# Fewer TensorE transposes of x, halved and paced loads, and tail groups that keep their own PSUM tile, in a fused attention and channel-mix kernel

## The chip, the cores and the metric

The kernel runs on one core of a Trainium2 chip. The metric is the time of one execution on the device in microseconds (us); lower is better. Executions of one kernel vary by about one per cent, so each comparison below uses several runs, with the kernel before run on the same chip in the same rounds. A run is called slow when it lies more than 1.5% above the fastest of the same kernel; ratios use the other ("fast") runs.

Engine names as the profile has them: PE is TensorE (matmul), PEld its weight loads, DVE is VectorE, ACT is ScalarE, POOL is GpSimd, SP is SyncE. A "q" behind an engine's name (SPq, POOLq) means its sequencer, which also issues DMAs.

## The reference, cut to what matters

```python
# q, k, v: (8, 8, 576, 64); features 128; d_model 512; d_ff 1024
def phi(x):
    proj = x @ w_phi
    proj = proj - max(abs(proj), axis=-1)
    return concat([exp(proj), exp(-proj)])
q_p, k_p = phi(q), phi(k)
x = (q_p @ (k_p^T v)) / (q_p @ sum(k_p) + 1e-6)      # heads side by side: (8, 576, 512)

x_prev = x shifted by one position
xk = mu_k * x + (1 - mu_k) * x_prev
xr = mu_r * x + (1 - mu_r) * x_prev
k = relu(xk @ w_k); v = (k * k) @ w_v; r = sigmoid(xr @ w_r)
out = r * v                                           # (8, 576, 512)
```

## The kernel before: the parts that matter here

The work is cut into 32 pairs of heads (four for each of eight batches), one tail group for each batch (three for the first; the ninth of the nine slices of 64 positions, for all heads together), and the channel mix of each batch. Each small operation has a name, and one long list of words says in which order they are emitted. Every engine and every DMA queue does its share in exactly this order. `kp20` is the projection of k of pair 20, `mh20` the copies of its maxima, `xz20` the DMA transposition of its x, `xu20` the copy behind it, `lk6.0` a load of k of batch 6. A suffix picks the engine (`/DVE`) or a PSUM tile (`:1`).

```python
ORDER = """
...
h2.1:1 rk15 kc14/ACT h2.2:0 nd13:2 rd13 xz13 xz13.d:0 lk6.0 rl2.1/ACT sq2.1/POOL mh15 rl2.2/ACT
sq2.2/POOL r2.0:1 th2.0 tr18 h2.3:0 so1.3.d:0 mt15:1 tr17 qp16:2 qp17:1 mc15/DVE rl2.3/ACT lq6.0
lv6.0 ka15 ea15 eb15 h2.4:0 h2.5:1 rq16 rq17 sq2.3/POOL rl2.4/ACT xu12/POOL df12/POOL qt15:2 qa15
...
"""
```

PSUM holds three tiles of two banks ("P", for projections, kv, nd) and two of one bank ("M", for h, r, v and small transposes). A tail group projects k and q into a P tile, has the maxima reduced on VectorE, copied on GpSimd (`mhe`), transposed by TensorE (`mte`), and then corrected by a matmul (`kae`) in the first bank. Its q part lies in an M tile:

```python
def mte():
    s["pm"] = pm = motile(("mo", "m" + tag), "ps_me")          # an M tile
    nc.tensor.transpose(pm[:, 0:64].bitcast(BF), mh, ident)
def kae():                                                      # the correction, bank 0 of the P tile
    nc.tensor.matmul(s["ps"][:, 0, 0:n * 128], lhsT=s["mT"][0:64, :],
                     rhs=sel[0:64, 0:n, :].rearrange("p a f -> p (a f)"),
                     start=False, stop=True, skip_group_check=True)
def qte():
    s["pq"] = ps = motile(("mo", "q" + tag), "ps_qe")           # another M tile
    ...
def eqe():                                                      # two exponentials from it (ACT)
    ...
    nc.scalar.activation(t[:, a0:a1, 64:192], s["pq"][:, 0:n * 128]..., AF.Exp, scale=...)
```

The output x of a pair reaches the channel mix transposed. Pairs 0 to 7 are transposed by TensorE, later ones by a DMA, behind which a 63-column copy shifts the edge:

```python
XPE = 8
def xz():
    nc.sync.dma_start_transpose(out=xs[:, a, :]..., in_=s["x"]...)
def xu(eng):
    copy(eng, xs[:, a, 1:64], xs[:, a, 576:639])
def mix(i):                                                     # always VectorE
    nc.vector.scalar_tensor_tensor(out=t[:, a, ...], in0=s["d"], scalar=mu[:, a:a + 1],
                                   in1=xs[:, a, 0:S], op0=ALU.mult, op1=ALU.add)
```

GpSimd issues all loads (q, k and v of a batch whole, 576 KB each, from batch 2 on), copies the maxima (`mhx`), and shares diffs and squares with VectorE and ScalarE.

## Time and profile before

| | before |
|---|---|
| time, median of 3 | 305.64 us (304.15 to 306.35) |
| profiled execution | span 304.2 us, mean granted clock 0.986 |
| TensorE / VectorE / ScalarE / GpSimd busy | 278.4 / 240.3 / 223.3 / 127.4 us |
| first h matmul starts | 51.9 us |

TensorE bounds the kernel, so the question in every stretch is what TensorE waits for. The prediction below shows the lines and how to read them. One more view: what TensorE's idle times ended with (line waited for, then us in total, times, longest). The kernel before has two of over 1.5 us in all:

```profile
PE ps_me L476 <- POOL mhlt L471: 3.5, 3, 2.4
PE ps_m L589 <- DVE ob L818: 1.6, 1, 1.6
```

What stands in no such line is the half rate after a gap and the crumbs too short to be listed.

### The profile page before, as it was taken

How to read it: one execution, taken by the hardware profiler on the slowest of the kernel's cores; microseconds unless marked ns; L12 is line 12 of the kernel's file. 1: busy time of each engine (PE TensorE's matmuls, PEld its weight loads, DVE VectorE, ACT ScalarE, POOL GpSimd, SP SyncE). 2: the span in 40 equal slices, each digit the busy share in tenths (PEclk: the TensorE clock that was granted, in tenths of full speed). 3: DMA queues.
4: the chain of work that ended last, by engine and by line, in shares of the span. 5: the costliest groups of instructions: out<-in, count | busy, mean ns of one | idle time of the engine just before them, and what ended most of it. 6: DMA issues, size and time to landing. Idle time of an engine off the chain costs nothing.

```text
span 304.2 us, 9054 instructions
## 1 busy us (share of the span) xinstructions
PE 278.4 (92%) x3765; PEld 158.4 (52%) x3813; DVE 240.3 (79%) x369; ACT 223.3 (73%) x408; POOL 127.4 (42%) x261
## 2 busy tenths in 40 slices
PE   6688798999899999969999997999999999999993
PEld 2456465565456655534555654454556655554541
DVE  5776789979978999667978988799869888777331
ACT  3397899998689897855888884898797878923410
POOL 7763533696047346653443714353034403400400
PEclk9999989999999999998999999999999999999999
DMA  8999957399989957996957898913924364233125
GB/s 152 204 209 207 169 83 105 59 194 206 194 174 128 148 124 131 197 200 113 177 110 107 145 125 157 162 47 61 187 60 69 11 93 94 58 74 71 39 58 116
DMA packets 66137, 38.18 MB, mean 126 GB/s; under 512 B 47024, under 2 KB 60720, under 8 KB 66096
## 3 DMA queue, kind: packets, MB, share of 16 engines
q1 hardware_dynamic: 51280, 20.82, 39.4%
q0 software_dynamic: 14672, 16.48, 35.1%
q8 instruction: 30, 0.49, 0.7%
q10 hardware_dynamic: 144, 0.29, 0.3%
q14 instruction: 11, 0.09, 0.1%
HBM read 33.62 MB, written 9.44 MB: 142 GB/s over the span
## 4 chain that ended last, share of the span: by engine, by line
PE 61%; DVE 18%; DMA 7%; ACT 6%; issue 3%; POOL 2%; SPq 1%; DVEq 0%; POOLq 0%
PE ps_v L812 14%; PE ps_h L779 13%; PE ps_r L798 7%; PE ps_nd L656 5%; DMA xs<-x_sc 4%; PE ps_kv L635 4%; DVE nm L565 4%; DVE nm L560 3%; DVE xk L706 2%; PE ps_ve L896 2%; ACT q L620 2%; PE ps_he L866 2%; DVE xr L706 2%; PE ps_q L548 2%; PE ps_k L598 2%
## 5 line engine op out<-in xcount | busy, mean ns | idle before, releaser
L620 ACT ACTIVATE q<-ps_qT 128x512 bf16<-128x512 f32 x128 | 67.1, 622 | 3.0 <-PE ps_qT L612 2.8
L575 ACT ACTIVATE k<-ps_k 128x1024 bf16<-128x1024 f32 x64 | 62.9, 1038 | 5.6 <-PE ps_k L598 4.3
L779 PE MATMUL ps_h<-xk,wk_bf 128*128 128x512 bf16 x237 | 60.8, 379 | 1.3 <-issue 0.3
L812 PE MATMUL ps_v<-wv_bf,kk 128*128 128x512 bf16 x243 | 58.2, 379 | 1.0 <-issue 0.3
L565 DVE TENSOR_REDUCE nm<-ps_q 128x8 f32<-128x1024 f32 x32 | 38.7, 1218 | 4.3 <-PE ps_q L548 4.1
L560 DVE TENSOR_REDUCE nm<-ps_k 128x8 f32<-128x1024 f32 x32 | 38.8, 1217 | 3.8 <-PE ps_k L548 3.8
L812 PEld LDWEIGHTS <-kk 128*128 128x128 bf16 x256 | 23.9, 98 | 28.8 <-issue 1.9
L211 POOL TENSOR_TENSOR kk<-krelu 128x512 bf16<-128x512 bf16 x23 | 23.9, 1047 | 35.4 <-DVE krelu L205 21.7
L779 PEld LDWEIGHTS <-wk_bf 128*128 128x128 bf16 x256 | 22.5, 97 | 25.2 <-issue 2.3
L584 POOL CAST mhl<-nm 128x16 bf16<-128x16 f32 x32 | 8.0, 250 | 64.1 <-DVE nm L560 64.0
L798 PE MATMUL ps_r<-wr_bf,xr 128*128 128x512 bf16 x118 | 32.9, 394 | 1.2 <-issue 0.5
L804 ACT ACTIVATE rt<-ps_r 128x512 bf16<-128x512 f32 x32 | 19.5, 609 | 18.0 <-PE ps_r L798 15.7
L700 POOL TENSOR_TENSOR diff<-xs 128x576 bf16<-128x576 bf16 x21 | 28.0, 1336 | 7.6 <-DVE xs L682 2.8
L203 ACT ACTIVATE krelu<-ps_h 128x512 bf16<-128x512 f32 x39 | 23.2, 611 | 10.1 <-PE ps_h L779 8.3
L706 DVE SCALAR_TENSOR_TENSOR xk<-diff,mu_k_t,xs 128x576 bf16<-128x576 bf16 x32 | 28.5, 892 | 1.3 <-POOL diff L700 1.0
L818 DVE SCALAR_TENSOR_TENSOR ob<-rt,ps_v 128x512 f32<-128x512 bf16 x32 | 21.8, 682 | 8.7 <-PE ps_v L812 4.2
L666 DVE TENSOR_TENSOR x_sc<-ps_nd,rden 128x640 bf16<-128x640 f32 x32 | 26.4, 825 | 1.1
L706 DVE SCALAR_TENSOR_TENSOR xr<-diff,mu_r_t,xs 128x576 bf16<-128x576 bf16 x32 | 26.9, 840 | 0.0
L548 PEld LDWEIGHTS <-qkT 64*128 64x128 bf16 x512 | 17.6, 94 | 12.0 <-issue 9.7
L635 PE MATMUL ps_kv<-v,k 64*128 64x65 bf16 x1024 | 22.8, 192 | 0.6 <-ACT q L620 0.4
L635 PEld LDWEIGHTS <-k 64*128 64x128 bf16 x1024 | 19.9, 95 | 5.1 <-issue 3.8
L205 DVE TENSOR_SCALAR krelu<-ps_h 128x512 bf16<-128x512 f32 x25 | 17.1, 688 | 6.6 <-PE ps_h L779 6.0
(99 smaller groups left out, 467.5 us busy)
## 6 DMA issues: line engine op xcount, KB each, us to landing
out_dram<-ob SPq DMA_DIRECT2D x72, 128.0 KB, 2.4
nat<-in_k_dram POOLq DMA_DIRECT2D x6, 576.0 KB, 8.6
nat<-in_q_dram POOLq DMA_DIRECT2D x6, 576.0 KB, 8.9
vt<-in_v_dram POOLq DMA_DIRECT2D x6, 576.0 KB, 9.6
wk_bf<-in_moe_w_k_dram POOLq DMA_DIRECT2D x2, 512.0 KB, 10.8
wv_bf<-in_moe_w_v_dram POOLq DMA_DIRECT2D x2, 512.0 KB, 12.3
nat<-in_k_dram POOLq DMA_DIRECT2D x3, 288.0 KB, 7.4
nat<-in_q_dram POOLq DMA_DIRECT2D x3, 288.0 KB, 7.3
```

Source lines behind the costliest of these rows:

```text
L211: (nc.vector if eng == "DVE" else nc.gpsimd).tensor_tensor(out_, in_, in_, op=ALU.mult)
L560: nc.vector.tensor_reduce(s["nm"][:, 0, :], s["k"].rearrange("p a (g f) -> p (a g) f", f=128), axis=AX.X, op=ALU.max, apply_absolute_value ...
L565: nc.vector.tensor_reduce(s["nm"][:, 1, :], s["q"].rearrange("p a (g f) -> p (a g) f", f=128), axis=AX.X, op=ALU.max, apply_absolute_value ...
L575: nc.scalar.activation(s[f"k{pn}"], s["k"].rearrange("p a (g f) -> p (a g) f", f=128), AF.Exp, scale=(1.0 if pn == 0 else -1.0))
L620: nc.scalar.activation(t[:, h, :].rearrange("f (g a p) -> f g a p", g=4, a=2), s["qT"].rearrange("f a (g h p) -> f h g a p", g=4, h=2)[:, ...
L635: nc.tensor.matmul(ps[:, hh, pn * 65:(pn + 1) * 65], lhsT=s[f"k{pn}"][r, c, :], rhs=vb[r, a, 2 * g + par, :], start=(pn == 0 and c == 0), ...
L666: nc.vector.tensor_tensor(s["x"].rearrange("p (b s) d -> p b s d", b=2), ndv[:, :, :, 0:64], s["rd"].to_broadcast([128, 2, 5, 64]), op=ALU ...
L700: (nc.vector if eng == "DVE" else nc.gpsimd).tensor_tensor(s["d"], xs[:, a, 64:64 + S], xs[:, a, 0:S], op=ALU.subtract)
L706: nc.vector.scalar_tensor_tensor(out=t[:, a, (b % 2) * S:(b % 2 + 1) * S], in0=s["d"], scalar=mu[:, a:a + 1], in1=xs[:, a, 0:S], op0=ALU.m ...
L779: nc.tensor.matmul(ps, lhsT=wk_bf[:, c, fc * 128:(fc + 1) * 128], rhs=xkt[bp][:, c, m0:m0 + 512], start=(c == 0), stop=(c == NDC - 1))
L798: nc.tensor.matmul(ps, lhsT=xrt[bp][:, c, m0 + ci * 128:m0 + (ci + 1) * 128], rhs=wr_bf[:, c, :], start=(c == 0), stop=(c == NDC - 1))
L812: nc.tensor.matmul(ps, lhsT=s["kk"][:, fc, ci * 128:(ci + 1) * 128], rhs=wv_bf[:, fc, :], start=(fc == 0), stop=(fc == NFC - 1))
```

## The change

The intent: less work on TensorE and ScalarE, more free PSUM tiles, loads that do not crowd the DMA transposes of x, and engines dealt out anew. The whole order was rewritten with it. Its core:

```diff
+    def pick(eng):
+        return nc.vector if eng == "DVE" else nc.gpsimd
...
-            "kpn": 2, "qpn": 2, "tl": 2, "xk": 2, "kk": 2, "krelu": 3, "rt": 3, "ob": 4,
+            "kpn": 3, "qpn": 3, "tl": 2, "xk": 2, "kk": 2, "krelu": 4, "rt": 4, "ob": 4,
...
+        pace = lambda i: [f"xu{4 * (b - 3) + i + (a0 > 0) * (1 if i > 3 else 2)}"] if b > 3 else []
...
-    lparts = {b: [(0, NP)] for b in range(B)}
+    lparts = {b: [(0, 2), (2, 4)] for b in range(B)}
...
         def mte():
-            s["pm"] = pm = motile(("mo", "m" + tag), "ps_me")
-            nc.tensor.transpose(pm[:, 0:64].bitcast(BF), mh, ident)
+            nc.tensor.transpose(s["ps"][:, 1, 0:64].bitcast(BF), mh, ident)
...
         def qte():
-            s["pq"] = ps = motile(("mo", "q" + tag), "ps_qe")
+            s["pq"] = ps = s["ps"][:, 1, :]
...
-    XPE = 8
+    XPE = 4
...
-                for h in range(2):
-                    nc.scalar.activation(
-                        t[:, h, :].rearrange("f (g a p) -> f g a p", g=4, a=2),
-                        s["qT"].rearrange("f a (g h p) -> f h g a p", g=4, h=2)[:, h],
-                        AF.Exp, scale=(1.0 if pn == 0 else -1.0))
+                nc.scalar.activation(t.rearrange("f j (a p) -> f j a p", a=2),
+                                     s["qT"].rearrange("f a (j p) -> f j a p", p=64),
+                                     AF.Exp, scale=(1.0 if pn == 0 else -1.0))
...
+                if eng == "POOL":
+                    md = small.tile([128, S], FP, name="md", bufs=1)
+                    nc.gpsimd.tensor_scalar(md, s["d"], mu[:, a:a + 1], None, op0=ALU.mult)
+                    nc.gpsimd.tensor_tensor(t[:, a, ...], md, xs[:, a, 0:S], op=ALU.add)
+                    return
...
+        cols = [(0, DM)] if bp < B // 2 - 1 else [(0, DM // 2), (DM // 2, DM)]   # last edge in halves
...
 ORDER: rewritten; for example, a tail group
- mce4.0/ACT ... kae4.0 ... ekt4.0 ... qte4.0:1 ... eqe4.0
+ mce4.0/DVE ... qte4.0 ... eqe4.0 ... kae4.0 ... ekt4.0
```

## The prediction

> **What bounds the kernel now.** I read the busy shares first, then the slices of the span, then the table of windows, then the chain that ended last, and then the order of time where the windows showed a hole. The page:
>
> ```profile
> PE 278.4 (92%) x3765; PEld 158.4 (52%) x3813; DVE 240.3 (79%) x369; ACT 223.3 (73%) x408; POOL 127.4 (42%) x261
> PE   6688798999899999969999997999999999999993
> PEclk9999989999999999998999999999999999999999
> ```
>
> TensorE is the bound: 92% busy, and from slice 7 on nearly always at nine tenths; no other engine passes 79%. But busy is not full speed, so I counted what TensorE had to do. In the chain eight 512-column matmuls take 1.73 us, 216 ns each; a pair's kv takes about 0.6 us, its nd 0.67, eight projections 0.23, one transpose of 128 columns 0.056. Counts times these spacings give 245 us of real work in 304. By windows of 8 us it is 25 us in the first 56 us (so 31 us are lost there), then 7.1 to 7.9 of 8 nearly everywhere, and only 4.9 and 5.9 in the two windows from 128 to 144. From 56 us to the end of the last matmul at 299.3 some 23 us are lost: some 4 us of it in those two windows alone (10.8 us of work where neighbours have 14.7), and the rest in crumbs of half a microsecond per window, with about 1 us extra each at 72, 168, 184 and 200. The table of windows there (columns: TensorE, its weight loads, VectorE, ScalarE, GpSimd, clock, DMA share, GB/s):
>
> ```profile
> 120.00:128.00 8.00, 7.89 (x116) 4.57 (x117) 5.45 (x9) 6.63 (x12) 4.21 (x7) 1.00 1.15 192
> 128.00:136.00 8.00, 5.51 (x103) 3.37 (x103) 5.66 (x8) 4.95 (x11) 4.96 (x10) 0.97 1.24 199
> 136.00:144.00 8.00, 7.51 (x46) 3.18 (x45) 5.88 (x10) 4.81 (x8) 3.08 (x11) 0.82 0.71 117
> ```
>
> And why, from the chain that ended last, and then from the order of time:
>
> ```profile
> 125.10 13.39 DMA xs<-x_sc
> ```
>
> ```profile
> 125.10 18.90 SPq L677 DMA_TRANSPOSE xs<-x_sc  x3
> 131.54 0.23 POOL L199 COPY xs<-xs 128x63 bf16<-128x63 bf16 x1 [2.80 <-DMA xs<-x_sc]
> 134.53 0.23 PE L476 MATMUL ps_me<-ident,mhlt 128*128 128x128 bf16 x1 [2.44 <-POOL mhlt L471]
> 137.98 1.06 PE L798 MATMUL ps_r<-wr_bf,xr 128*128 128x512 bf16 x2 [0.22 <-issue]
> ```
>
> GpSimd issued five whole loads of 576 KB between 117.5 and 127.7 us. In this stretch a transposing DMA of x needed 10.5 us in the median, against 3.5 us over the whole run. GpSimd stood in order behind it, the tail's small copies (mhlt) stood behind GpSimd, and TensorE stood behind those for 2.44 us. Then the clock was halved: the r matmuls that follow are 427 ns apart, for one stretch of 3.4 us.
>
> **What the Trainium skill says.** "DMA: Bandwidth & Descriptors", section "Issuing engines are not separate DMA queues": all DMAs end on the same 16 engines and interleave. The trace agrees: 10.5 against 3.5 us. "TensorE: Matmul & The Clock Gate", Part 1: an idle window of about 3.4 us brings half rate. The trace agrees on the half rate and its 3.4 us, though the visible gap was only 2.44 us. "ScalarE: Activation LUTs", section "What ACT_TABLE_LOAD costs": 186 ns + 0.833 ns per element, with 93 ns overlapped back to back: 612 ns for 512, 1039 for 1024. The trace has 622 and 1038. "GPSIMD Engine Reference", 4.1: operations with two inputs are about twice as slow on GpSimd as on VectorE. Here it is worse: the diff takes 1336 ns against 495.
>
> **The change, part by part.**
>
> (1) x of pairs 4 to 7 goes by DMA. Removed: 20 TensorE transposes, 20 x 0.056 = 1.1 us of work; four evictions, about 0.65 + 0.2 us each on ScalarE or VectorE, 3.4 us. Added: four DMA transposes of 3.5 us, with slack, since batch 1 is mixed only later. On the path: -1.1 us.
>
> (2) Loads of batches 2 to 7 are halved, and those of 4 to 7 stand in GpSimd's order behind the small copies that wait for x transposes landed before. Added: 18 more issues of 0.75 us on GpSimd, 13.5 us, off the path. The queue in front of a transpose becomes half as deep, so the hole at 128 to 144 should close. On the path: -4 us.
>
> (3) The tail groups put their small transpose and their q projection into the second bank of their own tile. This frees the two single banks twice for each of ten groups, for the h, r and v matmuls; the own tile is held about 1 us longer. Some of the crumbs: -0.5 us.
>
> (4) The two exponentials of q become one of 1024 elements each: 64 instructions less. By the two busy sums, 67.1 us for q and 62.9 us for k (which already has the one-piece form), ScalarE gains 4 us. It matters only in the head, where pairs take turns with ScalarE: -0.5 us.
>
> (5) Engines are dealt out anew. Counting each kind by its duration in the rows: VectorE loses 11 mixes (-9.5), 23 ReLUs and squares (-14), gains 7 diffs (+3.5), 11 copies of kv and mT (+3.4), and 26 groups of tiny maxima copies (+10, an estimate of mine at 0.15 us for each of 68 instructions): about -7, to 233 us. ScalarE: 13 ReLUs and five squares more, fewer copies, less for (4): about +4, to 227. GpSimd: 11 mixes of about 2.3 us each (estimate from its 1336 ns diff plus a one-input pass), so +25; loads +13.5, five squares +5, diffs -9.4, maxima copies -15: about +17 with small change, to 144. None becomes the bound. One wait shrinks: GpSimd's maxima copies, which stand between the reduction and TensorE, are for 18 of 32 pairs now on VectorE, directly behind the reduction. A third buffer for exponentials, kv and diff, and a fourth for ReLU and tanh, loosen more. Together: -1.5 us, half of it in the head.
>
> (6) The last edge product goes in two halves, its last stores from two queues.
>
> ```profile
> 297.34 1.89 PE L896 MATMUL ps_ve<-wv_bf,kke 128*128 128x512 bf16 x8
> 299.33 0.69 DVE L900 SCALAR_TENSOR_TENSOR ob<-rt,ps_ve 128x512 f32<-128x512 bf16 x1 [1.04 <-PE ps_ve L896]
> 300.04 1.10 SPq L905 DMA_DIRECT2D out_dram<-ob  x2
> ```
>
> Half the columns save about 0.28 us of the 0.69, and one issue of 0.55 us falls away: -0.8 us.
>
> (7) 16 warm-up matmuls more (55 for 39), 3.5 us, all before the first h, where TensorE has 31 us to spare: 0, or a little less where they keep the clock up (it was 0.79 from 32 to 40 us).
>
> Before the first h the work on VectorE is 43 us in both orders by my count, on ScalarE 41.5 before and 39 after, and the TensorE work still to come is 223 us in both. So the first h should start near where it did (53.0 us), perhaps 1 us sooner. Sum: 1.1 + 4 + 0.5 + 0.5 + 1.5 + 0.8 = 8.4 us, to **297 us**.
>
> **The rivals.** First, the hole is only moved. The new order still puts four half loads and a v close together around pairs 8 to 11, and four x transposes now run beside weight loads, which land in 10.8 to 12.3 us. An x transpose that is late holds GpSimd, and behind it a load, a square, or the fourteen maxima copies left there. For it: 13.4 us was seen. Against it: fewer maxima copies stand behind GpSimd, and the order leaves wide room before the copies of x. Time: 301 to 304. Second, GpSimd becomes the brake: 17 us more, and mixes of 2.3 us are on it in the head. It was 6 of 8 us busy up to 24 us already. Against it: 42% on average. Time: 299 to 303. Third, the load was never worth more than its own hole, and the new order simply has holes of its own: every order has about 19 us of crumbs, and a new one may have 16 or 23. That gives the width. Fourth, the new order is better all over, since deep buffers and short waits go with it: crumbs fall to 14 and the head by 3 us: 290 to 293.
>
> **Range and chances.** Faster by over 2% means under 299.5 us, only 2.5 us above my figure, which is less than what the crumbs may do. Slower than 311.8 would need a new hole of 15 us: hardly. I say 297, range 291 to 304; faster 0.65, within 2% 0.33, slower 0.02.
>
> **What would show it.** In the new profile: the windows from 120 to 150 us have TensorE near 7.8 and the clock at 1.00 (2); the longest wait for an x transpose in mid-run is under 8 us (2); 20 transposes into ps_x, not 40 (1); the q exponential takes about 1040 ns, 64 times (4); GpSimd is busy near 144 us and VectorE near 233 (5); from the last matmul's end to the end of the span 4.2 us rather than 5.0 (6); the first h starts at 51 to 54 us (5, 7). The prediction is wrong if the first h comes several microseconds earlier or later, or if the clock drops in mid-run again.

## The result

The changed kernel takes 318.35 us (median of 4 runs, 316.86 to 319.49) against 305.44 (4 runs, 304.15 to 306.35). The ratio is 1.042, with a 95% interval of 1.036 to 1.048: it is slower by 4%. Ratios in this document are the mean time of one kernel's fast runs over that of the other's of the same rounds, so not quite the ratio of the medians quoted. The prediction was 297 us, with two chances in a hundred for this side.

The page of the changed kernel, in the same rows as before:

```profile
PE 284.0 (90%) x3763; PEld 156.8 (49%) x3817; DVE 242.4 (77%) x422; ACT 226.8 (72%) x349; POOL 154.1 (49%) x233
PE   6877797999999499996999969999899999999995
PEclk9999599999999799999799999999999999999999
```

The last row, the clock granted to TensorE, has three dips, to 5 and 7 tenths, where it had two, to 8; the row above it, TensorE's busy tenths, shows a four and two sixes in mid-run. TensorE's work is almost the same: the prediction's 245 us, less 1.1 us for the 20 transposes of x that are gone. The difference is in holes. The windows, with the columns of the prediction:

```profile
32.00:40.00 8.00, 6.36 (x79) 2.97 (x82) 4.51 (x6) 2.85 (x4) 7.12 (x8) 0.57 1.23 208
104.00:112.00 8.00, 4.84 (x22) 1.73 (x23) 5.29 (x5) 3.22 (x5) 7.38 (x8) 0.79 0.74 113
128.00:136.00 8.00, 7.90 (x136) 4.87 (x135) 6.42 (x12) 7.79 (x12) 3.66 (x9) 1.00 1.17 149
136.00:144.00 8.00, 7.79 (x112) 4.13 (x113) 7.19 (x11) 7.62 (x13) 4.94 (x9) 1.00 0.97 146
144.00:152.00 8.00, 4.94 (x41) 2.27 (x39) 6.23 (x11) 6.06 (x11) 1.91 (x8) 0.99 0.48 96
152.00:160.00 8.00, 7.95 (x82) 3.61 (x83) 3.79 (x7) 2.73 (x5) 0.00 (x0) 0.80 0.33 68
184.00:192.00 8.00, 5.09 (x55) 2.70 (x55) 5.60 (x6) 4.41 (x8) 7.56 (x12) 1.00 0.77 134
```

The old hole at 128 to 144 us is closed, as predicted. But there are new ones at 104, at 144 to 160 (from 152 full by its busy time, yet at half clock for a part), and at 184. The head (the stretch before the channel mix begins) is worse too: the first h matmul comes at 55.5 us, not 51.9. (The prediction and the text of a2 have 53.0 and 55.6 for these; the traces have 51.92 and 55.45.) TensorE's waits:

```profile
PE ps_m L602 <- POOL mhl L598: 9.4, 4, 4.0
PE ps_e L495 <- ACT tq L517: 7.7, 7, 3.0
```

Both are new. The second is a matmul of the tail groups that waits for an exponential. In the order of time at 150.9 us it reads so (the changed kernel; start, length, what; in brackets the idle time before it and what ended it):

```profile
150.92 0.37 PE L495 MATMUL ps_e<-sel,mTe 64*128 64x512 bf16 x1 [3.01 <-ACT tq L517]
```

L495 is the correction `kae`, and L517 the exponentials of the q part, `eqe`. The correction writes bank 0 of the tail's tile, and the exponentials read bank 1. Neither needs the other. They wait because part 3 made them one tile, and because the new order puts `kae` behind `eqe` in seven of the ten tail groups; the list has seven such waits. In the kernel before, `kae` and `eqe` used different tiles.

The first wait, at 107 us, has another history. GpSimd's order, and then TensorE's:

```profile
103.34 0.23 POOL L210 COPY xs<-xs 128x63 bf16<-128x63 bf16 x1 [5.99 <-DMA xs<-x_sc]
105.55 0.74 POOL L597 CAST mhl<-nm 128x16 bf16<-128x16 f32 x1
107.10 0.23 PE L602 MATMUL ps_m<-ident,mhl 128*128 128x128 bf16 x1 [3.96 <-POOL mhl L598]
```

GpSimd had issued five half loads from 88.7 to 92.6 us. The DMA transposition of x issued at 92.5 took 10.8 us to land. GpSimd stood for 6 us at the 63-column copy that needs it, then did a load issue and a diff that come next in its order, and only then the 16-column copies of the maxima for which TensorE stood still. The same happens at 184 us, where the copy waits 4.8 us for a transposition.

### The profile page after: what moved, and what is told of

Read it like the earlier page. It is cut to its first block, busy times and chain, and to the rows that moved or that the text cites. A ratio compares the mean times of both kernels' runs of the same rounds, so it can differ in the third digit from the quotient of the medians.

```text
span 316.9 us, 9012 instructions
## 1 busy us (share of the span) xinstructions
PE 284.0 (90%) x3763; PEld 156.8 (49%) x3817; DVE 242.4 (77%) x422; ACT 226.8 (72%) x349; POOL 154.1 (49%) x233
## 4 chain that ended last, share of the span: by engine, by line
PE 58%; DVE 13%; DMA 13%; POOL 6%; issue 5%; ACT 4%; POOLq 0%; DVEq 0%; SPq 0%
PE ps_h L795 15%; PE ps_v L828 13%; PE ps_r L814 7%; DMA xs<-x_sc 5%; PE ps_nd L666 4%; DMA wr_bf<-in_moe_w_r_dram 4%; PE ps_kv L646 3%; DMA nat<-in_q_dram 3%; DVE nm L573 3%; DVE nm L578 2%; PE ps_ve L918 2%; PE ps_qT L619 2%; ACT k L588 2%; PE ps_k L611 2%; POOL nat L329 2%
## 5 line engine op out<-in xcount | busy, mean ns | idle before, releaser
L632 ACT ACTIVATE q<-ps_qT 128x1024 bf16<-128x1024 f32 x64 | 63.0, 1035 | 12.1 <-PE ps_qT L625 11.8
L828 PE MATMUL ps_v<-wv_bf,kk 128*128 128x512 bf16 x242 | 60.7, 391 | 1.0 <-issue 0.2
L222 POOL TENSOR_TENSOR kk<-krelu 128x512 bf16<-128x512 bf16 x26 | 27.1, 1051 | 51.2 <-ACT krelu L214 38.8
L214 ACT ACTIVATE krelu<-ps_h 128x512 bf16<-128x512 f32 x47 | 27.9, 609 | 11.0 <-PE ps_h L795 10.3
L820 ACT ACTIVATE rt<-ps_r 128x512 bf16<-128x512 f32 x32 | 19.2, 603 | 13.9 <-PE ps_r L814 13.7
L210 POOL COPY xs<-xs 128x63 bf16<-128x63 bf16 x24 | 6.6, 275 | 37.3 <-DMA xs<-x_sc 37.0
L720 DVE SCALAR_TENSOR_TENSOR xk<-diff,mu_k_t,xs 128x576 bf16<-128x576 bf16 x26 | 23.5, 904 | 0.4
L720 DVE SCALAR_TENSOR_TENSOR xr<-diff,mu_r_t,xs 128x576 bf16<-128x576 bf16 x27 | 22.8, 845 | 0.0
L646 PE MATMUL ps_kv<-v,k 64*128 64x65 bf16 x1024 | 21.8, 190 | 0.6 <-DVE x_sc L676 0.4
L666 PE MATMUL ps_nd<-kv,q 128*128 128x65 bf16 x512 | 21.4, 193 | 0.0
L709 POOL TENSOR_TENSOR diff<-xs 128x576 bf16<-128x576 bf16 x14 | 18.3, 1306 | 3.7 <-DVE xs L210 2.0
```

Of the source, the lines that this page charges most:

```text
L214: nc.scalar.activation(out_, in_, AF.Relu, scale=HALF)
L222: (nc.vector if eng == "DVE" else nc.gpsimd).tensor_tensor(out_, in_, in_, op=ALU.mult)
L632: nc.scalar.activation(t.rearrange("f j (a p) -> f j a p", a=2), s["qT"].rearrange("f a (j p) -> f j a p", p=64), AF.Exp, scale=(1.0 if pn ...
L646: nc.tensor.matmul(ps[:, hh, pn * 65:(pn + 1) * 65], lhsT=s[f"k{pn}"][r, c, :], rhs=vb[r, a, 2 * g + par, :], start=(pn == 0 and c == 0), ...
L666: nc.tensor.matmul(ps[:, bk, o * 65:(o + 1) * 65], lhsT=tail if sl < 2 else s[f"q{pn}"][:, sl - 2, :], rhs=s["kv"][:, sl % 2, pn, :], star ...
L720: nc.vector.scalar_tensor_tensor(out=t[:, a, (b % 2) * S:(b % 2 + 1) * S], in0=s["d"], scalar=mu[:, a:a + 1], in1=xs[:, a, 0:S], op0=ALU.m ...
```

## The experiments

Each experiment is an edit of the changed kernel ("changed + ...") or of the kernel before. All gave correct results. Kernels of one call share the runs of the kernel before: calls are a1 to a4; a5 to a7 with c1; a8, a9, b1 and b2; c2, c3, a10 and b3; c4; c5. Each call ran on another chip, so kernels of different calls are compared here by their ratios. Each kernel has one profile, of one of its runs.

My theory after reading the traces was that the loss is the sum of separate waits, above all that of the correction (part 3) and that of GpSimd's order behind x. The rivals were that GpSimd or VectorE has become the pace-maker (part 5), or that the head alone sets the time.

### a1: the correction ahead of the exponentials

```diff
 ORDER, in seven of the ten tail groups (the other three had it so already):
- qte4.0 ka16 ea16 df14/DVE eb16 eqe4.0 lk5.2.d:0 xa14/DVE kae4.0
+ qte4.0 kae4.0 ka16 ea16 df14/DVE eb16 eqe4.0 lk5.2.d:0 xa14/DVE
```

> The changed kernel; only the order within each tail group differs: the correction matmul into the first bank of the tail tile (kae) stands before the q exponential of that tile (eqe) and not behind it. Theory T (the shared tile makes the matmul wait for the exponential; trace of the changed kernel: 7 waits, 7.7 us, the longest 3.01 us at 151 us, after which 16 v matmuls took 5.31 us at half clock): the waits PE ps_e <- ACT tq vanish, the windows 144 to 160 are full, 313 to 314.5 us against 318. Rival (the wait only stands in for another one, the exponentials of k being late): the hole stays at the next matmul, 317 to 318.5.

Measured: 311.4 us (310.6 to 312.6), ratio 1.0148 (1.0081 to 1.0215), against 1.042. TensorE no longer waits for the exponentials of the tail. The windows of a1 at the place of the hole:

```profile
144.00:152.00 8.00, 7.63 (x88) 3.97 (x89) 7.59 (x14) 7.11 (x12) 1.56 (x8) 1.00 0.59 116
152.00:160.00 8.00, 7.95 (x84) 4.13 (x83) 7.45 (x12) 5.68 (x9) 3.47 (x6) 1.00 0.79 137
```

Moving one small matmul in seven tail groups gives back 7 us of the 13 by the medians, 8 by the ratios. The listed waits were 7.7 us.

### c1 and c2: part 3 alone on the kernel before, in two orders

```diff
 kernel before, tail groups in one P tile as in the change, and
- mce4.0 ... kae4.0 ... ekt4.0 ... qte4.0:1 ... eqe4.0
+ mce4.0 ... qte4.0 eqe4.0 kae4.0 ... ekt4.0            (c1)
+ mce4.0 ... qte4.0 kae4.0 eqe4.0 ... ekt4.0            (c2)
```

> The kernel before with part 3 of the change alone: the tail groups reuse their own tile, with the q part and its two exponentials ahead of the correction matmul as in the changed kernel. Theory (the correction waits for the exponentials because the tile is the same, some 3 us on TensorE for each of the later groups, and half clock after it): slower by 4 to 8 us, ratio 1.013 to 1.026, with waits of 2 us and more before the correction matmul, which the kernel before does not have. Rival (the wait hurts only beside the other parts of the change): within 1.5 us of the kernel before, ratio 0.995 to 1.005.

Measured for c1: 320.75 us (319.8 to 321.8), ratio 1.048 (1.044 to 1.052), far more than I had allowed. The wait is there, nine times, though none reaches the 2 us that I had expected:

```profile
PE ps_e L481 <- ACT tq L503: 9.7, 9, 1.2
```

> The kernel before with part 3 alone as in the run that was 15 us slower (ratio 1.048), but with the correction matmul ahead of the two exponentials of the q part. Theory A (all of it is the wait of the correction for exponentials that read the other bank of its tile): within 2 us of the kernel before, ratio 0.995 to 1.007, no wait of the correction for the exponentials. Theory B (the longer hold of the tile, one of three that the projections take turns with, costs by itself): ratio 1.015 to 1.035.

Measured for c2: 310.56 us, ratio 1.0144 (1.0119 to 1.017). It lies between what both theories expected. The order makes 10 us of the 15; the shared tile in the better order costs the other 4 to 5. Part of the 10 us is lost in the head: the first h matmul comes at 56.6 us in c1, 52.9 in c2 and 51.9 in the kernel before. For the rest of 4 to 5 us, c2 has waits of TensorE for a tile to be handed back by the tail's k exponentials:

```profile
PE ps_qT L604 <- ACT tk L488: 1.5, 2, 0.8
PE ps_k L546 <- ACT tk L488: 1.3, 2, 1.0
PE ps_nd L654 <- ACT tk L488: 1.3, 1, 1.3
PE ps_kv L633 <- ACT tk L488: 1.2, 1, 1.2
```

These are 5.3 us; the kernel before has 0.2 us of them. But c2's longest wait is another, and the old hole is deeper there than in the kernel before (7.51 us busy from 136 to 144):

```profile
PE ps_e L474 <- POOL mhlt L470: 4.9, 4, 3.8
136.00:144.00 8.00, 4.33 (x30) 2.36 (x32) 3.17 (x3) 3.20 (x8) 5.09 (x15) 0.79 1.25 183
```

So that the longer hold of the tile costs the 4 to 5 us is argued, not shown; a deeper old hole may be a part of it. In both runs the q part's two exponentials also come ahead of the k part's, so the tile is held longer for that reason too; c2 does not separate the two. Still, part 3 alone, in the better order, is a loss here.

### a2, a3, a4: the head, the maxima and the loads, each alone on the changed kernel

a2 moves two loads of batch 3 in GpSimd's order, since they held GpSimd at 30 us; a3 puts all maxima copies on VectorE; a4 issues the five half loads later, behind the copy of pair 9.

```diff
 changed kernel, ORDER
- lk3.0 lq3.0 qb1 ... xa0/POOL mt2:1 ekt0.2 xb0/POOL
+ qb1 ... xa0/POOL mt2:1 ekt0.2 xb0/POOL lk3.0 lq3.0                    (a2)
- mh0/DVE ... mh1/POOL ... mh2/POOL ... (14 of 32 on POOL)
+ mh0/DVE ... mh1/DVE ... mh2/DVE ...                                     (a3)
- lk4.0 ... lq4.0 lv3.0 ... lk4.2 ... lq4.2 ... xu8/POOL ... xu9/POOL
+ ... xu8/POOL ... xu9/POOL lk4.0 lq4.0 lv3.0 lk4.2 lq4.2                 (a4)
```

> The changed kernel; only GpSimd's order in the head differs: the two loads of batch 3 (k and q, first half), which stood in front of the maxima copies of pair 2 and waited there 2.8 and 0.4 us for loads issued eight earlier, are issued after the mixes of pair 0. Theory H (loads that wait in GpSimd's order delay the maxima copies, TensorE stands 2.6 us, the clock is halved from 33 to 40 us and the first h is at 55.6 instead of 53.0): the first h at 52 to 54, 315 to 316.5 us. Rival (the mixes of 3.1 us each on GpSimd are what delays the head): first h stays at 55 to 56, 317.5 to 318.5.

> The changed kernel; all 32 pairs' maxima copies on VectorE (18 are already). Theory G (GpSimd in its fixed order, behind x transposes that are late, behind load issues and behind its mixes, is what TensorE waits for through these copies, in the holes at 33, 104 and 186 us): these three holes shrink, 308 to 313 us although VectorE gets some 10 us more work. Rival V (VectorE is too full for it): holes move to the reductions, 316 to 321.

> The changed kernel; only the five half loads of batches 3 and 4 that GpSimd issues between 88.7 and 92.6 us (four halves of k and q, one of v) are issued after the copies of x of pairs 8 and 9. Theory B (this burst makes the x transposes of 89.6 and 92.5 us land after 7.5 and 10.8 us, and the GpSimd that waits for them makes the hole of 4 us at 103 to 107): those transposes land in 3 to 5 us, the hole goes, 312 to 314 us. Rival (the burst only moves and delays the transposes of pairs 10 and 11 or the q/k transposes of batch 4): 316 to 319.

Measured: a2 317.26 us, ratio 1.036 (1.028 to 1.044); a3 318.83, ratio 1.041 (1.032 to 1.051); a4 317.73, fast runs 311.2 and 315.3, two slow runs of 320, ratio 1.021 (1.008 to 1.033). a2 and a3 cannot be told from the changed kernel (1.042) while the wait of the correction is still in it; a4's fast runs are better, its slow ones not. In a2 the head did not become faster (first h at 55.1 us). In a3 it did: the first h comes at 52.6 us, not 55.5, and TensorE's wait of 2.6 us for GpSimd's copies at 33 us is gone. But a3 has holes of its own, at 80 to 88 us (4.95 us busy) above all, and ends no sooner. In a4 the hole at 104 us closed (7.49 us busy), but the profiled run, a slow one, had a new one at 80 to 88 us (3.81 us busy); a2's and a3's profiles have it as well, the changed kernel's own has not. In a4 it comes from the x transposition of pair 6, which part 1 added: it took 13.9 us there, against some 8 us in the changed kernel's own profile. So it seems that this kernel has a hole that comes and goes between runs; with one profile for each kernel that is not shown.

### a6 and a7: the mixes and the half loads

Both are made on top of a1. a6 has all 64 mixes on VectorE again. a7 has the loads of batches 2 to 7 whole again, each at the place of its first half.

```diff
 a1, and
- xa0/POOL xb0/POOL ... (11 of 64 mixes on POOL)
+ xa0/DVE xb0/DVE ...                                                     (a6)
-    lparts = {b: [(0, 2), (2, 4)] for b in range(B)}
+    lparts = {b: [(0, NP)] for b in range(B)}                            (a7)
```

> The correction-first kernel with all 64 mixes on VectorE, as in the kernel before. Theory (a mix on GpSimd costs 3.1 us there and holds everything behind it in GpSimd's order): GpSimd falls from 154 to about 131 us busy, VectorE rises by 6 us to about 248 us, the thin stretch at 176 to 192 us fills, and the time falls by 1 to 3 us, ratio 1.005 to 1.012. Rival (VectorE is already the engine that paces the pairs, so it is the dearer place): no change or slower by 1 to 2 us, ratio 1.015 to 1.022.

> The correction-first kernel with the loads of batches 2 to 7 whole again, each at the place of its first half; 18 fewer load instructions on GpSimd. Theory A (the halves were worth what the prediction gave them, about 4 us in the middle): slower by 2 to 4 us, ratio 1.022 to 1.028. Theory B (half loads double the number of issues, some 0.75 us of GpSimd each, 13 us in all, in front of the copies that TensorE waits for): faster by 1 to 3 us, ratio 1.005 to 1.012, with GpSimd's count of loads down by 18.

Measured: a6 312.73 us, ratio 1.0216 (1.0184 to 1.0248); GpSimd is busy 122 us there and VectorE 251. a7 310.6 us (307.4 to 311.3), ratio 1.0124 (1.0054 to 1.0194); GpSimd is busy 143 us, not 154. Against a1's 1.0148 the mixes on GpSimd cost nothing (taking them off is if anything slower), and halving the loads neither gives nor takes anything that these runs resolve. So GpSimd's amount of work does not look like what slows the kernel: 32 us less of it gained nothing in a6, where VectorE took over the work, and 11 us less, with nothing moved elsewhere, nothing that is resolved in a7. a7 also has the hole at 128 to 144 us closed (7.74 and 7.89 us busy), so the halving was not needed for that.

### a8, a9, a10: two places in GpSimd's order

On top of a1: a8 puts the maxima copies of two pairs, those that stood behind the late copies at 103 and 184 us, on VectorE. a9 issues the five half loads later (a4's edit). a10 is a9 with the maxima of pair 21 on VectorE.

```diff
 a1, and
- mh12/POOL ... mh21/POOL
+ mh12/DVE ... mh21/DVE                                                   (a8)
- lk4.0 ... lq4.0 lv3.0 ... lk4.2 ... lq4.2 ... xu9/POOL
+ ... xu9/POOL lk4.0 lq4.0 lv3.0 lk4.2 lq4.2                              (a9, a10)
- mh21/POOL
+ mh21/DVE                                                                (a10)
```

> The correction-first kernel (1.015 of before) with the maxima copies of two pairs alone, 12 and 21, on VectorE: in that kernel GpSimd had them standing behind a 63-column copy that waited 7.0 and 3.5 us for a DMA transpose of x, and behind a difference and a mix after it. Theory (TensorE's thin stretches at 96 to 112 and 176 to 192 us, 12 us of lost work there, come from GpSimd doing its work in order): both stretches fill by at least half, the waits of the transposes of the maxima for GpSimd vanish there, and the time falls by 3 to 6 us, ratio 0.995 to 1.005. Rival (the x of those pairs itself is late, so the wait only moves to the difference or to the h matmuls): within 1.5 us of 311.4, ratio 1.010 to 1.020.

> The correction-first kernel with the five half loads that GpSimd issued between 88 and 93 us put behind the copy of pair 9. Theory (these loads delay the DMA transposes of pairs 8 and 9, which hold GpSimd): the wait of 7.0 us at 96 to 103 us falls under 4 us, TensorE does at least 6 of 8 us of work in both windows from 96 to 112, ratio 1.004 to 1.010. Rival (they only move the queue to the next transposes or to the transposes of batch 4): ratio 1.012 to 1.018, with a new thin stretch after 112 us.

> The changed kernel with three places of its order mended: the correction ahead of the exponentials, the five half loads of 88 to 93 us behind the copy of pair 9, and the maxima of pair 21 on VectorE. The run without the third was at 306.5 us in its fast runs (0.998 of before), with 4.3 of 8 us of TensorE's work at 176 to 184 us behind a 5.1 us wait of GpSimd for a transposition. Theory: that stretch fills, 302 to 305 us, ratio 0.985 to 0.995. Rival (the hole only moves): 306 to 308 us, ratio 0.996 to 1.005.

Measured: a8 311.98 us, ratio 1.012 (1.001 to 1.022), fast runs from 308.4 to 312.5. Its profile, of a slow run, shows both old holes filled (7.68 and 8.00 us busy from 96 to 112, 8.00 from 176 to 184), but 3.84 us at 80 to 88 and 5.73 at 184 to 192: inconclusive as a time. a9 306.77 us, ratio 0.998 (0.989 to 1.006), with fast runs of 305.8 to 307.0 and a slow one of 314. Windows of a9:

```profile
96.00:104.00 8.00, 7.59 (x147) 4.59 (x143) 7.55 (x11) 6.02 (x10) 7.88 (x11) 1.00 1.01 170
104.00:112.00 8.00, 8.00 (x104) 4.90 (x102) 7.34 (x11) 5.72 (x8) 5.14 (x12) 1.00 1.27 175
```

In a1 the second of these windows was still a hole:

```profile
104.00:112.00 8.00, 5.37 (x32) 2.22 (x35) 5.02 (x5) 3.22 (x5) 6.88 (x7) 0.79 0.61 83
```

The copy of pair 9, which had waited 7 us in a1, now finds its x landed, as that of pair 8 does. With the two edits the changed kernel is level with the kernel before. The same edit, which gave 6 to 7 us in a4's two fast runs by the ratios and nothing in its two slow ones, gives 5 us once the correction is mended. a10 takes 305.82 us, ratio 0.999 (0.996 to 1.002): its window from 176 to 184 has 6.0 us busy instead of 4.7, and the time is not resolved from a9's. Time and ratio lie in the rival's range or just under it; that the hole moved is not shown.

### a5 and c3, c4, c5: part 1, the four x by DMA

a5 is a1 with x of pairs 4 to 7 transposed by TensorE again. I placed the transposes and evictions (the copies out of PSUM) by hand.

```diff
 a1, and
-    XPE = 4
+    XPE = 8
- xz6 ... xz6.d:0 ... xu6/POOL
+ xt6:1 xf6/ACT xe6/DVE            (behind th0.2; the other three likewise)
```

> The correction-first kernel (1.015 of before) with the x of pairs 4 to 7 transposed by TensorE again, as in the kernel before. Theory (the DMA transposes of these four pairs stand among the loads of the weights and of batches 2 and 3 and arrive 8 to 14 us after their issue, so TensorE runs dry between 56 and 100 us): the time falls by 2 to 5 us to a ratio of 1.000 to 1.008, and what TensorE does between 56 and 96 us is at least 7 of every 8 us. Rival (the thin stretches there come from the loads and the maxima on GpSimd, whoever transposes x): within 1 us of 311.4, ratio 1.012 to 1.018.

Measured: 320.44 us, ratio 1.0455 (1.0396 to 1.0514), 9 us slower than a1. Both expectations failed. Its trace has waits that my placement made: a transpose that waits 2.3 us for a tanh to free its bank, a VectorE eviction that waits 5.3 us for a ScalarE copy, the h matmuls 2.1 us for that eviction. So this run says nothing clean about part 1; it says what an unfitting placement costs. The clean direction is to add part 1 to the kernel before:

```diff
 kernel before, and
-    XPE = 8
+    XPE = 4
- rd6 ... xt6:0 sq0.7/POOL qt7:0 lk3.0.d:0 xf6/DVE xe6/DVE ... sq0.5/POOL ... mh8 ... df6/POOL
+ rd6 xz6 ... xz6.d:0 xu6/POOL ... sq0.5/POOL ... mh8 ... df6/POOL         (c3)
+ rd6 xz6 ... sq0.5/POOL ... mh8 ... xz6.d:0 xu6/POOL df6/POOL             (c4)
- tr3.0 so0.0 ... tr3.2 ... rd7 xz7
+ rd7 xz7 tr3.0 tr3.2 so0.0                                                (c5: c4 and this)
```

> The kernel before with part 1 of the change alone: x of pairs 4 to 7 by DMA transposes, copied by GpSimd. The prediction's step 1: faster by 1.1 us, ratio 0.994 to 0.999. Rival (the transposes stand among the loads of weights and of batches 2 and 3 and land 8 to 14 us after issue; the mixes of batch 1 and with them the h and r matmuls, and GpSimd's maxima behind the copies, come late): slower by 2 to 6 us, ratio 1.006 to 1.020, with TensorE under 7 of 8 us in one or two windows between 64 and 96 us.

Measured for c3: 320.58 us (319.7 to 321.9), ratio 1.0466 (1.0436 to 1.0495). Not 1.1 us faster, but 14 us slower, and more than the rival had it. Two lines of c3's order of time show the chain:

```profile
81.70 0.23 POOL L199 COPY xs<-xs 128x63 bf16<-128x63 bf16 x1 [8.34 <-DMA xs<-x_sc]
83.02 1.46 PE L812 MATMUL ps_v<-wv_bf,kk 128*128 128x512 bf16 x3 [7.42 <-POOL kk L211]
```

GpSimd stood 8.3 us at the copy of pair 6. The square (`kk`) for which TensorE waits stood right behind it. The Trainium skill ("Perfetto Trace Analysis", section "Per-instruction lifecycle: what the profiler-reported window actually captures") says that ScalarE, VectorE and GpSimd are strictly first in, first out. The trace agrees, and this decides the case: a 0.23 us copy that waits 8.3 us made TensorE wait 7.4 us for the square behind it.

> Part 1 alone on the kernel before, as in the run with ratio 1.047, but with GpSimd's copies of pairs 4 to 7 each directly ahead of the difference that needs them, so that a square and the maxima of two pairs are no longer behind the copy of pair 6, which waited 8.3 us for its transposition while TensorE waited 7.4 us for the square. Theory (part 1 costs through GpSimd's order): most of the 14 us come back, ratio 1.000 to 1.020, and TensorE's waits for GpSimd's square vanish. Rival (x itself is late, so that the h and r matmuls of batch 1 lack their mixes): ratio 1.035 to 1.050, with waits for mixes in place of the square's.

Measured for c4: 320.67 us, ratio 1.0507 (1.0454 to 1.0561). The theory fell. The wait for the square is gone and 72 to 80 us is full (7.50 us busy, before 3.33), but the hole came back at 88:

```profile
88.00:96.00 8.00, 2.05 (x22) 1.22 (x21) 3.36 (x5) 0.93 (x2) 0.87 (x3) 0.71 0.64 152
91.79 0.23 POOL L199 COPY xs<-xs 128x63 bf16<-128x63 bf16 x1 [9.43 <-DMA xs<-x_sc]
```

x of pair 7 itself is late. SyncE issues the transposes of x, of q and k, and the stores in one order, and pair 7's transposition stood behind two transposes of batch 3 and a store, which wait for loads and for an output; it was issued at 89.1 us.

> The kernel before with part 1 alone and GpSimd's copies late (ratio 1.051), and now also the transposition of pair 7's x issued ahead of the two transposes of batch 3's k and q and of the first store. In the run before, SyncE issued it at 89 us, 14 us after the others, and GpSimd waited 9.4 us for it while TensorE did 2 of 8 us from 88 to 96. Theory (part 1 costs because the added transposes are issued by one engine in order, behind transposes and stores that wait for other things): the transposition of pair 7 is issued before 80 us, the thin windows from 80 to 96 lose at most half as much, ratio 1.015 to 1.035. Rival (the cost sits elsewhere, as in the transposition of pair 6 that takes 13 us among loads): ratio 1.040 to 1.055.

Measured for c5: 314.43 us (312.7 to 315.5), ratio 1.030 (1.022 to 1.038). The copy of pair 7 waits 4.5 us instead of 9.4, and 88 to 96 us is busy for 6.70 us instead of 2.05. So 6 of the 15 us were SyncE's order. (x of pair 7 was issued a little after 80 us rather than before it.) The changed kernel has this transposition ahead of batch 3's, so it does not pay that part. How much of part 1's cost remains inside the changed kernel is not settled by these runs.

### b1, b2, b3: what the kernel before can take from it

b1 is the kernel before with the merged q exponentials (part 4). b2 moves the loads of batch 6, which crowd the hole at 128 to 144 us. b3 has both, and the last edge in halves (part 6).

```diff
 kernel before, and (b2, b3)
- xz13 lk6.0 ... lq6.0 lv6.0 ... xu15/POOL ... xu16/POOL
+ xz13 ... xu15/POOL lk6.0 lq6.0 ... xu16/POOL lv6.0
```

> The kernel before with part 4 of the change alone: one exponential over 1024 columns instead of two over 512, for q. The prediction's step: 64 fewer instructions, 4 us less of ScalarE, and a time lower by 0.5 us, ratio 0.996 to 1.000, q exponentials of about 1.04 us. Rival (ScalarE has slack, so nothing): ratio 0.998 to 1.003. Slower than 1.004 would say that the merged instruction reads or writes in a worse order for TensorE's loads of q.

> The kernel before with the loads of batch 6, issued by GpSimd at 119 and 126 us, put behind the copies of pairs 15 and 16 (about 145 and 160 us). The prediction's step 2 (the hole at 128 to 144 us is made by loads in the way of the DMA transposes of x and is worth 4 us): the transposition of pair 12 falls from 13.4 us to under 8, TensorE does at least 7 of 8 us in the windows 128 to 144, and the time falls by 3 to 5 us, ratio 0.984 to 0.991. Rival (another transfer or the next in order takes the place): ratio 0.995 to 1.005, with the hole there or further on.

> The kernel before with the three things of the change that are expected to help, and nothing else: merged q exponentials (0.990 alone), the loads of batch 6 later (0.985 alone in its fast runs), the last edge in halves over two queues (predicted -0.8 us). If they add, 299 to 301.5 us, ratio 0.975 to 0.984, with a tail of about 4.2 us after TensorE's last matmul against 5.0. Rival (the first two fill the same hole, so they do not add): 302 to 303.5 us, ratio 0.985 to 0.990.

Measured: b1 304.43 us (303.6 to 305.0), ratio 0.990 (0.982 to 0.999). By the medians it gains 1.4 us; the interval is wide because the kernel before had a run of 309.1 that counts as fast in those rounds. b2 304.87 us with two levels, 302.0 and 302.8, and 307.0 and 307.6, which count as slow; ratio of its two fast runs 0.985 (0.974 to 0.995). The hole is closed in its profiled run, of 302.0 us:

```profile
128.00:136.00 8.00, 7.64 (x120) 4.28 (x113) 7.59 (x12) 7.13 (x15) 5.90 (x16) 1.00 0.17 35
136.00:144.00 8.00, 8.00 (x104) 4.25 (x103) 7.01 (x11) 5.52 (x10) 5.87 (x12) 1.00 0.64 101
```

The transposition of pair 12 was no longer behind loads: the DMA engines moved 35 GB/s there instead of 199. The two fast runs lie 3 to 4 us under the median of the kernel before, about what the prediction gave to this hole. But only two of b2's four runs did so; the median of all four is 0.9 us under that of the kernel before. b3, over five rounds: 304.57 us (302.4 to 307.2), ratio 0.992 (0.989 to 0.995). It beats both kernels, the kernel before by some 2 us, but the parts do not add: 302.4 is its fastest run, at a mean granted clock of 1.00, and the others are at 0.985 to 0.994. In its profile the windows from 120 to 144 are full, and a thinner stretch has come at 152 to 160 (6.14 us busy) and 176 to 184 (6.87), as in b2. Its tail, from the last matmul's end, was shortened only to 4.65 us, not to the expected 4.2: SyncE was still issuing the stores before:

```profile
295.99 0.42 DVE L906 SCALAR_TENSOR_TENSOR ob<-rt,ps_ve 128x256 f32<-128x256 bf16 x1 [0.52 <-PE ps_ve L899]
296.10 1.83 SPq L914 DMA_DIRECT2D out_dram<-ob  x3
```

## Why the prediction was wrong, step by step

**What held.** The hole at 128 to 144 us closed in the changed kernel (7.90 and 7.79 us busy at clock 1.00), and two of b2's four runs gain about what step 2 gave it. But the halving, from which step 2 expected it, was not needed: with whole loads the hole is closed as well (a7). There are 20 transposes into ps_x, 64 q exponentials of 1035 ns, and the last edge's tail is 3.8 us:

```profile
311.16 1.91 PE L918 MATMUL ps_ve<-wv_bf,kke 128*128 128x256 bf16 x16
313.10 0.42 DVE L925 SCALAR_TENSOR_TENSOR ob<-rt,ps_ve 128x256 f32<-128x256 bf16 x1 [0.40 <-PE ps_ve L918]
313.56 0.55 ACTq L933 DMA_DIRECT2D out_dram<-ob  x1
```

This is 1.2 us less than the 5.0 of before; step 6 said 0.8. Step 4 was of the right size or too small (1.4 us for b1, in an interval that leaves room for 0.5). One reading of the prediction needs a word: as an estimate from the 186 ns and 0.833 ns per element of the Trainium skill's page "ScalarE: Activation LUTs" (section "What ACT_TABLE_LOAD costs"), exponentials of 512 and 1024 elements take 612 and 1039 ns if the overlap is left out, and these are what the trace's 622 and 1038 agree with.

**Step 3 failed, and is the largest part.** It read: "This frees the two single banks twice for each of ten groups"; "the own tile is held about 1 us longer"; "-0.5 us". It looked at which tiles come free, and not at what now shares a tile. The correction got a wait for exponentials that it does not need: 7.7 us of listed waits, 7 us of time (a1), and part 3 alone costs 15 us in the kernel before in such an order (c1). Even in the better order the shared tile costs 4 to 5 us (c2) instead of gaining 0.5; the longer hold, which I had named and not priced, is a likely part of that. The new order shows `kae` behind `eqe`; I had it before predicting and did not ask what that does to a shared tile.

**Step 2 failed as a sum, by the first rival.** The prediction gave -4 us for the hole and trusted that "the order leaves wide room before the copies of x". The rival had it: "An x transpose that is late holds GpSimd, and behind it a load, a square, or the fourteen maxima copies left there." The five half loads at 88 us did just that; issuing them later gave 5 us once the correction was mended (a9 against a1). Halving, undone alone, changed nothing that is resolved (a7). The check promised, that no x transposition takes over 8 us in mid-run, failed with 10.8.

**Step 5 was wrong in its size, but not where it mattered.** GpSimd came to 154 us, not 144, since a mix there takes 1.73 to 1.85 us for its product and 1.31 to 1.40 for its sum, together some 3.1 us, not 2.3. VectorE came to 242, not 233, since a maxima copy takes 0.35 us there on average, not 0.15. Neither made a new bound: moving the mixes back did not help (a6), nor did the maxima alone (a3). The second rival, GpSimd as the brake by its amount of work, finds no support in them.

**Step 1** said -1.1 us "with slack, since batch 1 is mixed only later". It priced four transpositions at 3.5 us each and nothing that stands behind them. Added alone to the kernel before it costs 14 to 15 us, of which SyncE's order of issue is 6 (c3 to c5). In the changed kernel its own cost is open: the only run that takes it out (a5) brought waits of its own.

**The head**, step 5's "half of it in the head" and "perhaps 1 us sooner", came 3.5 us later (55.5 against 51.9 us). At 30 us GpSimd waited 2.8 us to issue a load with the maxima copies behind it, TensorE waited 2.6 us for these, and its clock was at 0.57 from 32 to 40. With all maxima copies on VectorE the first h comes 2.9 us sooner (a3), with the correction first 1.2 us sooner (a1; 54.3 us). Moving the loads did not mend it (a2): TensorE's wait at 33 us is gone there, but it waits 2.2 us for VectorE at 41 us and has a clock of 0.59 from 40 to 48. a3 waits 1.9 us at that place and keeps a clock of 1.00. So the place of the maxima copies is likely the larger part of the head's delay; how it divides is open.

**The account.** Of the 13 us lost, the order of the correction is 7 (8 by the ratios) and the crowded loads are 5. With both mended the kernel is level with the one before (a9, 0.989 to 1.006), so nothing of the loss is left that these runs resolve. What stays open is the gain of 8.4 us that did not come: that the hold of the tile, the later head and perhaps part 1 eat what parts 2, 4 and 6 give is argued, not measured.

The range failed too. "Slower than 311.8 would need a new hole of 15 us: hardly" treated the new holes as one event. Three holes of about 3 us of idle time each, at 104, 144 and 184 us, two of them with half clock behind, and a head that is 3.5 us later are enough.

## What to carry to other kernels

When a change lets two uses share a tile, list every pair of instructions on that tile and check which comes first in each engine's order: a wait appears between instructions that touch different banks, even though neither needs the other. A small copy that waits for a DMA on an in-order engine is as costly as whatever stands behind it, so put such copies behind the work that the bound engine waits for, and space the loads around the transfers that such copies need. An order that is tuned as a whole does not take or lose one part without being refitted: undoing or adding part 1 here cost 9 us (a5) and 14 us (c3), with waits that the placement made, so test a part in both directions before crediting it.

## What the Trainium skill lacked or had wrong

- No page I read says that instructions on different banks of one PSUM tile wait for each other in such a kernel: the correction waited up to 3.0 us for exponentials from the other bank, and putting it first removed all such waits (a1). The profile infers who ended a wait from semaphore signals, which points to the kernel's bookkeeping by tile rather than to the hardware; no run here tells the two apart.
- "TensorE: Matmul & The Clock Gate", Part 1, has half rate after an idle window of about 3.4 us. Here half rate also followed visible gaps of 3.01 us (150.9 us in the changed kernel, window clock 0.80) and 2.62 us (33.3 us, window clock 0.57). But it did not follow gaps of 3.01 us in a3 (150.3 us) and 3.21 us in a9 (179.3 us), where the windows have a clock of 1.00, so the length of the visible gap alone does not decide.
- "GPSIMD Engine Reference", 4.1, has two-input operations about twice as slow on GpSimd as on VectorE: here 1306 ns against 496 for the diff, 2.6 times. Its product with a per-partition scalar, one tensor input with an fp32 result, took 1729 to 1853 ns for 576 elements, longer than the two-input diff, where the same row has one-input operations at roughly line rate.
- No page I read gives the time of one DMA transposition of a 128 x 640 tile next to other transfers: here 2.6 us at the quickest (c4) and 10.8 to 13.9 us at the slowest, among loads (10.8 in the changed kernel, 13.4 in the kernel before, 13.9 in a4). A plan that takes the median of 3.5 us for it is wrong where it matters.
